# Fewer blocks of 256 rows and more of 512, partly beside the routing, in a convolution and mixture-of-experts kernel

## The chip, the cores and the metric

The kernel runs on one core of a Trainium2 chip. The metric is the device time in microseconds of one execution. Three runs of the kernel before gave 1305.73 (the median), 1305.75 and 1302.89 us. A fourth execution was profiled: it took 1303.41 us, of which the span from the first to the last instruction is 1301.4.

The engines are named as in the profile: PE (TensorE, matrix products; PEld are its weight loads), DVE (VectorE), ACT (ScalarE), POOL (GpSimd, which also issues the scattering transfers) and SP (which issues the plain transfers). A lower-case q (SPq) marks an engine's sequencer. Each engine works through its own list of instructions in order.

## The reference

A causal convolution with softmax weights per head comes first, then a mixture of eight experts, one per token:

```python
# x (8, 3584, 192), 8 heads of 24 channels, 7 taps; w = softmax(weight)
out = einsum('hk,bskhg->bshg', w, windows_of(x))      # convolution
# mixture of experts on the result, D = 192, E = 8, F = 1024
logits = x @ w_gate
local_gate = sigmoid(x @ w_local)
for b in range(B):
    for s in range(S):
        fresh_e = argmax(logits[b, s])
        e = fresh_e if s == 0 or local_gate[b, s] < 0.5 else prev_e
        prev_e = e
        p = softmax(logits[b, s])
        h = maximum(x[b, s] @ w1[e], 0)
        out[b, s] = p[e] * (h @ w2[e])
```

All is in 32-bit floats. There are 28672 tokens. Each keeps the expert of the token before it unless its local gate is below one half, so the choice of expert runs along each sequence.

## The kernel before

**Routing.** The tokens are cut into 16 parts of 1792. For each part, `conv` computes the convolution (per head one product on ACT, L402, then six multiply-and-adds on DVE, L412: 48 a part). `logits` transposes the result on DVE (L595), multiplies it by the gate on PE (L605), copies the products to SBUF on ACT (L610), transposes them again (L613) and puts them in place with 16 small copies on DVE (L621). `route` is then a long row of small DVE instructions which find each token's expert and its place among that expert's tokens. The tokens' rows are scattered by `put` (L802) to a list in DRAM, one list per expert in units of 128 rows: 14 scatters a part, issued by POOL. `table` (L815) computes for a kind of block which expert and which units the blocks of that kind take. A "part" in the change's description is such a part; the parts are counted from 0 in the code.

**Blocks.** The experts' work is done in blocks of rows which all belong to one expert: `blocks` (L919) is the list of them in the order in which PE does them. A single has 128 rows, a pair 256, a block of four 512. A block loads its rows (`load_rows`, 97.5, 195 or 390 KB) and its expert's weights (`load_w`, 1536 KB), both issued by SP three blocks ahead. How many blocks of a kind are surely full after so many parts is known before the run (`_sure`); where a number is only probable (`_likely`, with the rows left over set by LEFT4 and the like), spare blocks at the end make up for a wrong guess. By the constants, before has 28 singles, then 63 pairs, then, when all parts are routed, 13 blocks of four, 4 pairs and 15 singles, with 18 spare singles behind a branch.

**How a block is computed.** For singles and pairs up to the end of the 63 (`FIRST` blocks), `turn` transposes the next block's rows on PE and copies them with ACT to xT, `hidden` does 24 matmuls of 256 columns (for a pair; 64 of the array's rows each, two halves side by side), ACT's relu makes hT, and `output` does 32 matmuls of 192 columns, one scaling by the token's probability on ACT and one on DVE (L1031), and a scatter of each 128 rows to the output by POOL (L1035). From `FIRST` on, `banks.close()` gives the PSUM banks to the late form. There a block of four does its hidden layer by `seven`: sums and differences of halves of the weights (`combine_w`, four POOL subtractions) and of the rows (`combine_x`, five DVE instructions), 44 matmuls of 256 columns instead of 48, and three DVE additions (L1167, L1170, L1180) with relus. `output_late` then does the output in two parts of 256 rows.

**The order of the work.** It is written out by hand: the program's order is each engine's order. Between the pieces of a block, `step(time)` emits instructions of `route` and `conv` until their estimated costs reach `time`. A generator yields its cost after each instruction (0.6 for a convolution's, 0.2 for a small one), or "hop" to give way to the convolution for the rest of that step. Per pair there are steps of 4.8, 1.2 and 3.6. `put` emits one scatter, if one is waiting, and can hang it behind an instruction, so that scatters stand apart. `ensure(i)` loads the rows up to three blocks ahead, and if the parts needed two blocks ahead are not routed or not put, it emits the routing at once. There are no steps in the late form before the change: everything is routed by then.

**Buffers.** Row tiles (y_sb) rotate over four; in the late form the two x tiles and a row tile hold the transposed rows, their combinations, the combined weights and the hidden pieces (`make_room`, L1052), and another row tile is a ring of four blocks' rows (`ring`).

The lines that set the cost of a pair and of a block of four:

```python
        if i < FIRST:
            hT = hidden(n, wbs[i], xT, (1, 1) if i else (0, 0))
            ...
            step(2.4 if i == 0 else 2.1 if n == 1 else 4.8)
            output(n, wbs.pop(i), xgs.pop(i), hT)
            ...
            step(1.3 if n == 1 else 3.6)
            continue
        ...
        if n == KQ:
            hT, at, wt = seven(wbs[i], wt, xT, xc, turn_next, weights_next)
```

Of the kernel before, what the change touches and what calls it, by code (L numbers as in the profile page):

```python
# [17 lines left out]
P = 128  # L18
# [5 lines left out]
UT = 128  # L24
# [41 lines left out]
PAIRED = 63  # L66
LEFT4 = E * (QT // 2 + UT // 8)
LEFT2 = E * (BT // 2 + UT // 8)
# [3 lines left out]
PAST = ONE[-1] * UT + TWO[-1] * BT  # L72
FOUR = _likely(N - PAST, QT, LEFT4)
LOST = FOUR - _sure(N - PAST, QT)
# [7 lines left out]
REST = NU - ONE[-1] - 2 * TWO[-1] - 4 * FOUR - 2 * PAIRS + LOSE  # L82
# [21 lines left out]
def kernel(  # L104
# [14 lines left out]
    ys = ctx.enter_context(tc.tile_pool(name="ys", bufs=4))  # L119
# [5 lines left out]
    hp = ctx.enter_context(tc.tile_pool(name="hp", bufs=1))  # L125
    op = ctx.enter_context(tc.tile_pool(name="op", bufs=2))
# [244 lines left out]
    tab = [cst.tile([P, 3], F32, name=f"tab{k}") for k in range(5)]  # L371
    ends = [cst.tile([P, 1 + E], F32, name=f"ends{k}") for k in range(5)]
    for k in range(5):
        nc.gpsimd.memset(tab[k], 0.0)
        nc.gpsimd.memset(ends[k], 0.0)
# [12 lines left out]
    def row_tile():  # L388
        return ys.tile([P, NB, DG], F32, name="y_sb")

    def conv(g, x_sb):
        y_sb = row_tile()[:, :NT, :]
# [197 lines left out]
    def logits(g, y_sb):  # L590
# [6 lines left out]
        yield "hop"  # L597


        lps = [hps_p.tile([P, TQ * Q], F32, name="hps") for half in range(2)]  # L600
# [14 lines left out]
        lt = sm.tile([P, NT + 2, E + 1], F32, name="lt")  # L615
        for r in range(4):
            for j in range(4):
                t, u = TQ * j, min(TQ * (j + 1), NT)
                at = r // 2 * TQ + t - begin[j]
                e0 = r % 2 * (E + 1)  # L620
                nc.vector.tensor_copy(lt[Q * r:Q * r + Q, t:u, :],  # L621
                                      lq[Q * j:Q * j + Q, at:at + u - t, e0:e0 + E + 1])
                yield 0.12
        return lt

    def route(g):
# [62 lines left out]
        krow = sm.tile([1, 2, P], F32, name="krow")  # L689
# [89 lines left out]
    def tables(g):  # L779
        if ONE[g] > (ONE[g - 1] if g else 0):  # L780
            yield from table(0, g, 1, ONE[g])
        if TWO[g] > (TWO[g - 1] if g else 0):
            yield from table(1, g, 2, TWO[g])
        if g == LAST:
            yield from table(2, g, 4, FOUR, 0)
            yield from table(3, g, 2, PAIRS, 0)
            yield from table(4, g, 1, None)
            yield from fill(g)
# [133 lines left out]
    blocks += [(2, 4, i, LAST) for i in range(FOUR)]  # L922
    blocks += [(3, 2, i, LAST) for i in range(PAIRS)]
    blocks += [(4, 1, i, PADS) for i in range(REST)]
# [40 lines left out]
    def turn(n, xg):  # L965
# [9 lines left out]
        xT = tp.tile([P, KD, BT], F32, name="xT")  # L975
# [13 lines left out]
    def hidden(n, wb, xT, shares=(1, 1)):  # L989
# [4 lines left out]
        for two in range(2):  # L994
            hps = [hps_p.tile([P, 2, BT], F32, name="hps") for half in range(2)]
            for d in range(KD):
                for j in range(2):
                    f0 = (d * 4 + two * 2 + j) * P
                    for half, rows in halves():
                        nc.tensor.matmul(hps[half][:, j, w], lhsT=wb[rows, f0:f0 + P],  # L1000
                                         rhs=xT[rows, d, w], start=(d == 0 and j == 0),
                                         stop=(d == KD - 1), skip_group_check=True)
# [7 lines left out]
    def output(n, wb, xg, hT):  # L1010

        yps = [yps_p.tile([P, 512], F32, name="yps") for half in range(2)]
        for m4 in ([0, 1, 4, 5], [2, 3, 6, 7]):
            for k in range(n):
                for m in m4:
                    for half, rows in halves():
                        nc.tensor.matmul(yps[half][:, k * D:(k + 1) * D],  # L1017
                                         lhsT=hT[rows, m, k * P:(k + 1) * P],
                                         rhs=wb[rows, WA + m * D:WA + (m + 1) * D],
                                         start=(m == 0 and k == 0), stop=(m == FK - 1),  # L1020
                                         skip_group_check=True)
        o_sb = op.tile([P, KT, D], F32, name="o_sb")
        y = [[yps[half][:, k * D:(k + 1) * D] for half in range(2)] for k in range(n)]
        for k in range(n):
            half = nc.scalar.activation(o_sb[:, k, :], y[k][0], Act.Copy, scale=xg[:, k, 0:1])  # L1025
        if n == KT and len(to_put) > NT - 2:
            put(half)

        step(1.2 if n > 1 or st["block"] else 0)
        for k in range(n):  # L1030
# [3 lines left out]
            nc.gpsimd.nop()  # L1034
            sent = nc.gpsimd.indirect_dma_start(  # L1035
                out=out, in_=o_sb[:, k, :], in_offset=None,
                out_offset=bass.IndirectOffsetOnAxis(ap=xg.bitcast(I32)[:, k, IX:], axis=0),
                bounds_check=N - 1, oob_is_err=False)
            tc.declare_no_dep(sent.ins, group="sent", reason="each token has one slot")
            tc.add_to_no_dep_group("sent", sent.ins)  # L1040
# [4 lines left out]
    def ring(i):  # L1045

        if "rows" not in room:
            room["rows"] = row_tile().rearrange("p b d -> p (b d)")
# [3 lines left out]
    def make_room():  # L1052

        one, two = [xs.tile([P, NX, D], F32, name="x_sb").rearrange("p t d -> p (t d)")
                    for _ in range(2)]
        three = row_tile().rearrange("p b d -> p (b d)")
        for name, flat, at, size in (("xT", one, 0, KD * QT), ("xc", one, KD * QT, 4 * HU * P),
                                     ("wt", one, KD * QT + 4 * HU * P, 6 * P),
                                     ("h0", two, 0, 4 * HU * P), ("h1", two, 4 * HU * P, 4 * HU * P),
                                     ("h2", two, 8 * HU * P, 4 * HU * P), ("h3", three, 0, 4 * HU * P)):  # L1060
            room[name] = flat[:, at:at + size]
# [13 lines left out]
    def turn_in(n, at):  # L1075
        xT = room["xT"][:, :KD * n * P].rearrange("p (d s) -> p d s", d=KD)
# [34 lines left out]
    def combine_w(wb):  # L1111


        wt = room["wt"].rearrange("p (k s) -> p k s", k=3)
# [397 lines left out]
```

## Time and profile before

| what | value |
|---|---|
| three runs | 1305.73 us median, 1302.89 to 1305.75 |
| the profiled execution | 1303.41 us |
| its span | 1301.4 us, mean granted PE clock 0.997 |
| last convolution instruction on DVE | ends at 799.9 us |
| last of the 63 pairs on PE | ends at 902.9 us |
| blocks of four on PE | 902.9 to 1168.4 us (13 x 20.42) |

The page of the profile shows for each engine its busy time, and then the span in 40 slices of 32.5 us, one digit each for the busy share in tenths. In the timeline a line gives the start, the length, the engine, the line of the kernel, the operation, its output and inputs, and how many instructions are merged. A matmul on 32-bit floats leaves two records. PE's ends are modelled, so the starts of its instructions are what to measure between. In the table of stretches, each engine has its busy time and, in brackets, its number of instructions. Two more groups, to see what scatters and copies cost:

```profile
L802 POOL DMA_INDIRECT slots<-y_sb,posi x228 | 229.7, 1007 | 203.3 <-ACT xT L986 86.3
L402 ACT ACTIVATE y_sb<-x_sb,c 128x336 f32<-128x336 f32 x112 | 61.7, 578 | 0.0
```

After the number of instructions stand the busy time in us, the mean of one in ns, and the idle time of the engine before them with what ended most of it.

### The profile page before, as it was taken

The numbers are of one execution on the slowest core, as the hardware profiler recorded it, in microseconds if no ns is written. First come the engines' busy times: TensorE is split into PE (matmuls) and PEld (weight loads), VectorE is DVE, ScalarE is ACT, GpSimd is POOL, SyncE is SP. The second block draws the span as 40 slices with busy tenths as digits, with TensorE's granted clock in tenths as the row PEclk, the third lists the DMA queues.
The fourth block names the chain that finished last, engine by engine and source line by source line (L and its number), as shares of the span: only waits on it lengthen the run. The fifth ranks groups of instructions, "written<-read, shape, count | busy, mean of one in ns | idle before, by whom it ended". The sixth has DMA issues, their size and how long they took to land. (4 is left out here: it accounts for less than half of the span.)

```text
span 1301.4 us, 40454 instructions
## 1 busy us (share of the span) xinstructions
PE 1283.3 (99%) x16290; PEld 1218.0 (94%) x16290; DVE 844.9 (65%) x2507; ACT 647.4 (50%) x1458; POOL 523.0 (40%) x577
## 2 busy tenths in 40 slices
PE   8899999999999999999999999999999999999997
PEld 7799999999999999999999999999999999999997
DVE  6989898888989899999998986812333333320000
ACT  5456564545544454444544444344565645544443
POOL 4455352434435344453544535455433343321111
PEclk9999999999999999999999999999999999999999
DMA  5899998757757576675766756556232323324684
GB/s 198 285 353 414 390 387 319 269 189 262 261 207 277 190 278 244 217 275 202 275 238 239 272 202 217 201 209 239 87 120 106 138 92 132 132 85 170 224 320 172
DMA packets 62210, 295.67 MB, mean 227 GB/s; under 512 B 11968, under 2 KB 33783, under 8 KB 44994
## 3 DMA queue, kind: packets, MB, share of 16 engines
q1 hardware_dynamic: 39696, 247.82, 52.7%
q0 software_dynamic: 22320, 45.22, 9.5%
q8 instruction: 130, 2.13, 0.7%
q14 instruction: 62, 0.51, 0.1%
q10 hardware_dynamic: 2, 0.00, 0.0%
HBM read 247.40 MB, written 46.07 MB: 226 GB/s over the span
## 5 line engine op out<-in xcount | busy, mean ns | idle before, releaser
L1017 PE MATMUL yps<-wb,hT 64*128 64x192 f32 x4928 | 426.4, 326 | 2.2 <-DVE o_sb L1031 2.2
L1000 PE MATMUL hps<-xT,wb 64*128 64x256 f32 (+1 forms) x4368 | 421.2, 345 | 1.7 <-DVE at L504 1.2
L1017 PEld LDWEIGHTS yps<-wb,hT 64*128 64x128 f32 x4928 | 403.3, 188 | 3.7 <-DVE o_sb L1031 2.5
L1000 PEld LDWEIGHTS hps<-xT,wb 64*128 64x128 f32 x4368 | 372.3, 187 | 34.7 <-issue 3.6
L412 DVE SCALAR_TENSOR_TENSOR y_sb<-x_sb,c,y_sb 128x336 f32<-128x336 f32 x672 | 375.6, 570 | 28.0 <-ACT y_sb L402 10.0
L802 POOL DMA_INDIRECT slots<-y_sb,posi x228 | 229.7, 1007 | 203.3 <-ACT xT L986 86.3
L1005 ACT ACTIVATE hT<-hps 128x512 f32<-128x512 f32 (+1 forms) x364 | 173.7, 529 | 243.4 <-PE hps L1000 243.3
L1035 POOL DMA_INDIRECT out_dram<-o_sb,xg x154 | 160.4, 1041 | 276.4 <-DVE o_sb L1031 219.0
L1210 DVE SCALAR_TENSOR_TENSOR o_sb<-ps,y_sb,o_sb 128x192 f32<-128x192 f32 x75 | 28.5, 414 | 238.9 <-ACT o_sb L1207 238.9
L1215 POOL DMA_INDIRECT out_dram<-o_sb,y_sb x75 | 77.4, 1032 | 240.9 <-DVE o_sb L1210 230.2
L1197 PE MATMUL ps<-wb,x_sb 64*128 64x192 f32 x1984 | 167.9, 324 | 0.0
L1197 PEld LDWEIGHTS ps<-wb,x_sb 64*128 64x128 f32 x1984 | 162.0, 187 | 0.6
L1025 ACT ACTIVATE o_sb<-yps,xg 128x192 f32<-128x192 f32 x154 | 57.8, 417 | 179.8 <-PE yps L1017 179.8
L986 ACT COPY xT<-xps 64x256 f32<-64x256 f32 (+3 forms) x364 | 138.9, 382 | 10.6 <-PE xps L384 5.1
L1031 DVE SCALAR_TENSOR_TENSOR o_sb<-yps,xg,o_sb 128x192 f32<-128x192 f32 x154 | 58.0, 410 | 73.4 <-ACT o_sb L1025 73.3
L1207 ACT ACTIVATE o_sb<-ps,y_sb 128x192 f32<-128x192 f32 x75 | 28.2, 417 | 103.5 <-PE ps L1197 99.0
L1153 PE MATMUL ps<-x_sb,wb 64*128 64x256 f32 x624 | 73.8, 376 | 0.0
L1153 PEld LDWEIGHTS ps<-x_sb,wb 64*128 64x128 f32 x624 | 59.1, 187 | 7.2
L1104 PE MATMUL ps<-x_sb,wb 64*128 64x128 f32 (+1 forms) x912 | 64.6, 294 | 0.1
L1104 PEld LDWEIGHTS ps<-x_sb,wb 64*128 64x128 f32 x912 | 62.1, 188 | 1.4 <-issue 0.7
L402 ACT ACTIVATE y_sb<-x_sb,c 128x336 f32<-128x336 f32 x112 | 61.7, 578 | 0.0
L1084 ACT COPY x_sb<-xps 64x512 f32<-64x512 f32 (+6 forms) x128 | 59.8, 467 | 2.4
(277 smaller groups left out, 1040.5 us busy)
## 6 DMA issues: line engine op xcount, KB each, us to landing
wb<-in_w_dram SPq DMA_DIRECT2D x119, 1536.0 KB
x_sb<-in_x_dram SPq DMA_DIRECT2D x14, 1920.0 KB
xg<-slots SPq DMA_DIRECT2D x63, 195.0 KB
wb<-in_w_dram SPq DMA_DIRECT2D x12, 512.0 KB
y_sb<-slots SPq DMA_DIRECT2D x13, 390.0 KB
slots<-y_sb,posi POOLq DMA_INDIRECT x228
x_sb<-in_xb_dram SPq DMA_DIRECT2D x4, 768.0 KB
xg<-slots SPq DMA_DIRECT2D x26, 97.5 KB
```

Source lines behind the costliest of these rows:

```text
L402: nc.scalar.activation(cols(h), chans(h, 0), Act.Copy, scale=c[:, h, 0:1])
L412: nc.vector.scalar_tensor_tensor(cols(h), chans(h, k), c[:, h, k:k + 1], cols(h), Alu.mult, Alu.add)
L802: ins = nc.gpsimd.indirect_dma_start(out=slots[:, :], in_=rows, in_offset=None, out_offset=bass.IndirectOffsetOnAxis(ap=to, axis=0)).ins
L986: copied = nc.scalar.copy(a, b)
L1000: nc.tensor.matmul(hps[half][:, j, w], lhsT=wb[rows, f0:f0 + P], rhs=xT[rows, d, w], start=(d == 0 and j == 0), stop=(d == KD - 1), skip_g ...
L1005: relu = nc.scalar.activation(hT[:, m:m + 2, w], hps[half][:, :, w], Act.Relu)
L1017: nc.tensor.matmul(yps[half][:, k * D:(k + 1) * D], lhsT=hT[rows, m, k * P:(k + 1) * P], rhs=wb[rows, WA + m * D:WA + (m + 1) * D], start= ...
L1035: sent = nc.gpsimd.indirect_dma_start(out=out, in_=o_sb[:, k, :], in_offset=None, out_offset=bass.IndirectOffsetOnAxis(ap=xg.bitcast(I32)[ ...
L1104: nc.tensor.matmul(hps[:, half, j, :], lhsT=wb[rows, f0:f0 + P], rhs=xT[rows, d, :], start=(d == 0 and j == 0), stop=(d == KD - 1), skip_g ...
L1153: ins = nc.tensor.matmul(to[:, half, j, :], lhsT=b[rows, j * P:(j + 1) * P], rhs=a[rows, :], start=(first and j == 0), stop=True, skip_gro ...
L1197: ins = nc.tensor.matmul(yps[:, half, k * D:(k + 1) * D], lhsT=h[two][rows, side, j, k * P:(k + 1) * P], rhs=wb[rows, WA + f * D:WA + (f + ...
L1215: sent = nc.gpsimd.indirect_dma_start(out=out, in_=o_sb[:, k, :], in_offset=None, out_offset=bass.IndirectOffsetOnAxis(ap=xg.bitcast(I32)[ ...
```

## The change

The 63 pairs become 44. After them come 18 blocks of four which are taken as the parts are routed (parts 9 to 14, table kind 2, cumulative numbers 1, 4, 8, 11, 15, 18 in `MID`), then 4 more when all is routed, 5 pairs and 15 singles, with 14 spare singles. The routing thus runs on beside the late form. For that:

- `seven` and `output_late` get steps of their own, `SIDE` = 2.4, 5.4, 2.0 and 1.8: ahead of the addition to h11, ahead of the output, and ahead of the DVE scalings of each of the two output parts. What a step overran is taken off the next (`over`), and in the late form each routing instruction is charged 0.05 more.
- The logits' products on PE need a PSUM tile. In the late form they use one of the block's own (`bank`), behind the first output part, at the earliest a block after their transposes were emitted ("pe" in place of the first "hop").
- From the seventh part on (`aside`), the 16 small copies of `logits` go to ACT, four at a time with a "hop" after each four.
- The second scatter of each 256 rows of output is held back (`held`) and hung behind a matmul of the next block; some puts hang behind matmuls instead of ACT instructions; puts in the late form move.
- The late form no longer takes x tiles: its pieces lie in the tile that `hots` used, in five small row tiles and in hT. Row tiles rotate over four up to part 7 and over three from then on.
- `combine_x` is cut in two so that its last two results can wait for hT in the first block of four; `ensure` is called inside `seven`.

The diff, cut:

```diff
-PAIRED = 63
+PAIRED = 44
+LEFTM = E * (QT // 2 + UT // 2)
...
+MID = [_likely((g + 1) * PT - PAST, QT, LEFTM) if TWO[g] == TWO[-1] else 0
+       for g in range(LAST)]
...
-    def row_tile():
-        return ys.tile([P, NB, DG], F32, name="y_sb")
+    def row_tile(g):
+        at = g % 4 if g < NARROW else (g + 1) % 3
+        return ys[at].tile([P, NB, DG], F32, name="y_sb")
...
-        yield "hop"
-        lps = [hps_p.tile([P, TQ * Q], F32, name="hps") for half in range(2)]
+        yield "pe"
+        if late_p:
+            both = st["bank"].tile([P, 2, 512], F32, name="ps")
+            lps = [both[:, half, :TQ * Q] for half in range(2)]
+        else:
+            lps = [hps_p.tile([P, TQ * Q], F32, name="hps") for half in range(2)]
...
+        aside = g > EARLY + 2
...
-                nc.vector.tensor_copy(lt[Q * r:Q * r + Q, t:u, :],
-                                      lq[Q * j:Q * j + Q, at:at + u - t, e0:e0 + E + 1])
-                yield 0.12
+                if aside:
+                    nc.scalar.copy(dst, src)
+                else:
+                    nc.vector.tensor_copy(dst, src)
+                    yield 0.12
+            if aside:
+                yield "hop"
...
+        if MID[g] > (MID[g - 1] if g else 0):
+            yield from table(2, g, 4, MID[g], MID[g - 1])
...
+            if k == 0:
+                deliver(o_sb[:, 0, :], xg, 0)
+            else:
+                held.append(lambda ins, k=k: deliver(o_sb[:, k, :], xg, k, ins))
...
-    def seven(wb, wt, xT, xc, turn_next, weights_next):
+    def seven(wb, wt, xT, xc, rows_then, turn_next, weights_next):
...
-        times(yb, s1, t1, True)
+        ins = times(yb, s1, t1, True)
+        if held:
+            held.pop(0)(ins)
+        rows_then()
...
+        if st["block"] > FIRST:
+            step(SIDE[0], early=1)
         nc.vector.tensor_tensor(h11, wbk, h11, op=Alu.add)
...
+            if n == KQ:
+                step(SIDE[2 + part], late_p[0] if part == 0 else None)
...
+    SIDE = (2.4, 5.4, 2.0, 1.8)
...
-    def step(time):
+    def step(time, bank=None, early=0, force=False):
...
+        if st["due"]:
+            go = (not late_p and st["block"] < FIRST - 1
+                  or bank is not None and (force or st["since"] < st["block"]))
+            if go:
+                st["due"], st["bank"] = False, bank
+        time += st["over"]
...
-                time -= c
+                time -= c + 0.05 if go and late_p else c
+        st["over"] = min(time, 0) if late_p else 0
...
+        if n == KQ:
+            step(SIDE[1])
```

## The prediction

> **What bounds the kernel now.** I read the page's engine lines and slices first, then TensorE's timeline in the middle and in the late stage, then the busy times of single blocks, then VectorE beside GpSimd. The chain of waits is of no use here: it holds only the last scatter.
>
> ```profile
> PE 1283.3 (99%) x16290; PEld 1218.0 (94%) x16290; DVE 844.9 (65%) x2507; ACT 647.4 (50%) x1458; POOL 523.0 (40%) x577
> PE   8899999999999999999999999999999999999997
> DVE  6989898888989899999998986812333333320000
> ```
>
> TensorE is full from the second slice to the last. VectorE is nearly full up to slice 27 of 40 (about 850 us; convolution and routing) and lightly used after. So the end moves only if TensorE gets less work, or if VectorE makes it wait.
>
> TensorE's timeline, first two blocks of 256 rows, then one of 512 (start, length, line, count of records; a matmul leaves two records):
>
> ```profile
> 613.06 5.42 PE L1017 MATMUL yps<-wb,hT 64*128 64x192 f32 x64
> 618.32 5.35 PE L1000 MATMUL hps<-xT,wb 64*128 64x256 f32 x48
> 623.50 0.40 PE L384 MATMUL xps<-ident,xg 64*128 64x64 f32 x8
> ...
> 634.39 5.42 PE L1017 MATMUL yps<-wb,hT 64*128 64x192 f32 x64
> ```
> ```profile
> 943.75 2.75 PE L1153 MATMUL ps<-x_sb,wb 64*128 64x256 f32 x24
> ...
> 949.79 1.89 PE L1153 MATMUL ps<-x_sb,wb 64*128 64x256 f32 x16
> 951.52 0.64 PE L384 MATMUL xps<-ident,y_sb 64*128 64x64 f32 x16
> 951.99 1.08 PE L1153 MATMUL ps<-x_sb 64*128 64x256 f32 x8
> ...
> 964.17 1.03 PE L1153 MATMUL ps<-x_sb,wb 64*128 64x256 f32 x8
> ```
>
> Two blocks of 256 rows take 634.39 - 613.06 = 21.33 us, without a gap. The block of 512 takes 964.17 - 943.75 = 20.42. It does the same rows with 44 hidden matmuls of 256 columns (`seven`) in place of 48. The gain is 0.91 us for each 512 rows.
>
> Busy times over one such stretch each (length, then PE, PEld, DVE, ACT, POOL):
>
> ```profile
> 602.40:623.73 21.33, 21.33 (x247) 20.09 (x243) 19.55 (x86) 10.08 (x24) 8.08 (x9) 1.00 0.52 183
> 943.75:964.17 20.42, 20.42 (x234) 19.24 (x234) 7.01 (x12) 11.24 (x15) 7.20 (x8) 1.00 0.33 117
> ```
>
> Beside two pairs VectorE is already 19.55 of 21.33 busy, of which only four scalings (2 x 0.74) belong to the blocks. A block of 512 brings 7.0 us of its own, so 13.4 are left for routing there.
>
> **What the Trainium skill says.** "TensorE: Matmul & The Clock Gate", Back-to-back issue gap: a warm matmul follows the last after N/2.4 + 2.5 ns. That is 109 ns for 256 columns; the trace has 48 records in 623.50 - 618.32 = 5.18 us, so 108. Hence TensorE's time is its columns, and four matmuls (eight records) less are 0.87 us by the page, 0.91 by the trace, which I use. The same page, under "Architectural detail: the array is 16× 32×32, not 1× 128×128", says that ScalarE and VectorE are strict first in, first out; a late instruction delays everything written behind it (no row of before shows that at a price, as VectorE is never late for TensorE in mid-kernel). "SBUF — State Buffer", Who interferes with whom: a VectorE instruction with two SBUF inputs and a GpSimd instruction that reads SBUF exclude each other. This trace shows it, on VectorE and on GpSimd, in the one place where such work meets:
>
> ```profile
> 900.61 0.93 DVE L1131 TENSOR_TENSOR x_sb<-x_sb 128x256 f32<-128x256 f32 x1 [1.21 <-ACT x_sb L1084]
> 901.58 0.84 DVE L1132 TENSOR_TENSOR x_sb<-x_sb 128x256 f32<-128x256 f32 x1
> 902.45 0.83 DVE L1133 TENSOR_TENSOR x_sb<-x_sb 128x256 f32<-128x256 f32 x1
> ...
> 961.06 0.42 DVE L1131 TENSOR_TENSOR x_sb<-x_sb 128x256 f32<-128x256 f32 x1
> ```
> ```profile
> 901.34 0.79 POOL L1120 TENSOR_TENSOR x_sb<-wb 128x256 f32<-128x256 f32 x1
> 902.21 0.80 POOL L1122 TENSOR_TENSOR x_sb<-wb,x_sb 128x256 f32<-128x256 f32 x1
> ```
>
> Beside GpSimd the same subtraction takes 0.83 to 0.93 us instead of 0.42: about 0.44 lost for each GpSimd subtraction met.
>
> **The change part by part.**
>
> *Blocks on TensorE.* By the constants, before has 28 singles, 63 pairs, 13 blocks of 512, 4 pairs, 15 singles (the last 18 are spare and skipped). After has 28, 44, 18 + 4, 5, 15. In the instructions, 256-column hidden matmuls fall from 2180 to 2144, which is 9 x 4; all else on TensorE is unchanged in sum, logits included. 9 x 0.91 = **8.2 us less**. The blocks beside routing are filled by a guess of how many whole units exist (LEFTM); a wrong guess would run empty blocks. Counted from the reference's own choices for these inputs, the tables at parts 9 to 14 find 3, 5, 11, 12, 15, 20 such units where 1, 4, 8, 11, 15, 18 are asked, and 15 singles remain in both kernels. So the change does what it says, and no spare runs.
>
> *VectorE in sum.* Nine more blocks of 512 for 18 pairs: 9 x 7.0 - 18 x 0.74 = +50 us. Four more tables (13 in place of 9) of some 4 us each (L821 to L884 in the timeline at 617.8): +16. Logit copies of ten parts leave: 160 x 0.2 = -32. Net +34 on 845, beside TensorE. As it has 80 us idle between 215 and 850 (554.73 of 635 busy) and more later, the sum hides; only its place can hurt.
>
> *VectorE in each late block.* With the order of instructions in the changed kernel and durations from the rows of before (convolution 0.583 us apart: 14 in 8.18), routing and convolution in the 16 blocks of 512 that carry any come to 9.2 to 12.1 us in the ten full ones (heaviest the sixth, with the transposes of the logits), and 0 to 8.3 in the rest. So a full block has 7.0 + 10.9 = 17.9, heaviest 19.1, of 20.42. To that comes the meeting with GpSimd: four `combine_w` subtractions per block, which so far mostly lay beside an idle VectorE. Lower bound 0 (beside additions from PSUM), nearest row 0.44 each, upper bound their whole 0.73: 0 to 2.9 us per block; I take 1.8. Full blocks are then at 19.7, the heaviest at 20.9.
>
> *Where a late VectorE stops TensorE.* In the late block from its start: the addition to h11 can begin at 5.46 (949.21), the one to h22 ends at 7.8, and at 8.24 (951.99) the next product into that PSUM tile needs it. That leaves 0.43 us. Ahead of h11 in the queue now stand the last scaling of the block before (from 0.95), 1.7 us of routing ahead of that, and 2.3 behind it. Fed at full rate, VectorE is at 9.2 after h12, does 7 us plus 1 to 1.5 of meeting, two scalings at about 18, `combine_x` to 20.5, routing to 22.2 (1.8 of the next block), scalings to 2.5, routing to 4.8: h11 is in time by 0.6. A convolution also waits for ScalarE's first product of its head (L402), which in this place stands behind the four xT copies ending at 14.0 (957.78): up to 1 us in some blocks. In the sixth block it and the 8.1 us of its side work push h11 to about 6.7, and TensorE stops for some 1 us. I take 1 for this, 0.3 for each of five other full blocks: **2.5 us of stalls**; bounds 0 and 8.
>
> *Copies of logits on ScalarE.* From the seventh part on, 16 a part; ScalarE does 64x128 in 0.26 and 64x256 in 0.365, so a 36-element one is about 0.18: 2.9 us a part, four at a time. In pairs ScalarE idles 50% and has free stretches of 2 us; the cover is those. In late blocks it goes from 11.2 by 1.1 (L402) and 0.7 to 13 of 20.4. Zero; if one group falls ahead of a copy of h11, whose slack is 1.3 us, a few tenths.
>
> *GpSimd.* 36 more subtractions (26 us) and puts, now behind matmuls. A late block holds 4 x 0.74, four deliveries and five puts at about 1.3 each: 14.6 of 20.4. The second delivery of a block waits for a product of the next; behind it stand puts, for which the row loads on SP wait. The loads are two blocks (40 us) ahead, so zero. The same holds for the first of the four groups of the last part: its rows are loaded in the 17th late block and turned in the 18th.
>
> *Buffers.* The 512-row blocks move from the x buffers to others (hot, small xg tiles, hT), and row tiles rotate over three from part 8; the start of convolution g already required that g-3 was put. Zero. Weight loads fall by nine; DMA is 0.3 to 0.9 busy. Zero.
>
> Sum: 1301.4 - 8.2 + 2.5 = 1295.7 span; with the 2.0 us around it (1303.41 - 1301.4) 1297.7. The profiled execution lies 2.3 under the median of the runs and 0.5 over the fastest; their mean is near 1304.4, 1298.7 from there. I forecast **1298**.
>
> **Rivals.**
> *The stalls take the gain.* Each of the ten full blocks loses 0.7 us, by meeting GpSimd near the upper bound and L402 late each time: 7 of the 8.2, so 1303. For it: only 0.43 us of slack. Against: blocks with tables and light routing, where VectorE recovers.
> *Slower: VectorE becomes the bound of the late blocks beside routing.* Its place is the in-order queue ahead of h11. If a full block costs it 7.0 + 11.6 (the planner's own quota, 2.4 + 5.4 + 2.0 + 1.8) + 2.9 + 0.5 of waits for ScalarE = 22.0, then the ten full blocks are each 1.6 over TensorE's 20.42: +16 - 8.2, about 1312 from the mean of the runs. The lead of the routing then cannot help, for the delay sits in the block's own additions. It decides from 8.2 / 10 = 0.82 us per block on. For it: 19.55 of 21.33 was busy already, with less work of the blocks. Against: the quota overstates small operations (routing L697 to L774: 8.1 us measured for 9.4 charged).
> *No stalls at all*: 1301.4 - 8.2 + 2 = 1295; inside the forecast's case.
>
> **How the numbers follow.** What a measurement of this kernel tells from no change is about 0.3%, 3.9 us. Forecast with zero to 4 us of stalls: 0.71, at 1294 to 1301. Gain eaten: 0.15, at 1301 to 1307. Slower: 0.14, above 1308, most near 1312. Faster is the first case and 0.01 of the second, 0.72; the same 0.13; slower 0.15 with the top of the second. The range is 1294 to 1304: below it 0.04, above it 0.15 at most.
>
> **What would show it.** Late blocks of 20.4 us from about 700 us on (902.91 - 19 x 10.67), 22 of them; TensorE's idle time within them under 4 us, ended by VectorE's addition to h11 or h22, mostly in the sixth and seventh; VectorE at 18 to 20 us in full blocks, its convolutions or `combine_x` stretched where GpSimd subtracts. Periods of 21 us or more in many blocks, or gaps where rows are waited for, would prove it wrong.

## The result and the profile after

Of each kernel there are twenty runs. The kernel before took 1304.5 us (median, 1301.84 to 1307.87), the changed kernel 1300.88 (1297.88 to 1304.85). The ratio is 0.9971, with a 95% interval from 0.9962 to 0.9979. The forecast was 1298, its range 1294 to 1304. The profiled execution of the changed kernel has a span of 1296.3 us, against 1301.4 before: 5.1 less in the two profiles, 3.6 in the two medians. The changed kernel's profiled execution, 1298.23 us, is the second lowest of its twenty.

The page after, its engine lines and the two slices that were shown of before:

```profile
PE 1276.7 (98%) x16218; PEld 1232.7 (95%) x16218; DVE 909.4 (70%) x2513; ACT 704.0 (54%) x1573; POOL 546.0 (42%) x615
PE   9899999999999999999999999999999999999997
DVE  6989898888888888798888888988468434310000
```

TensorE is busy 6.6 us less and is full as before. VectorE now works up to slice 32 (about 1040 us): its row stays at 8 where it was at 9, so the routing is stretched over more of the span, as the change intends.

TensorE's timeline, one late block (a block of 512 rows) beside routing; its first line is the block's start, its last the start of the next:

```profile
694.20 2.76 PE L1194 MATMUL ps<-xT,wb 64*128 64x256 f32 x24
...
702.43 1.09 PE L1194 MATMUL ps<-xT,xg 64*128 64x256 f32 x8
703.35 1.03 PE L1194 MATMUL ps<-xT,wb 64*128 64x256 f32 x8
704.22 10.57 PE L1243 MATMUL ps<-wb,hot 64*128 64x192 f32 x128
714.62 2.76 PE L1194 MATMUL ps<-xT,wb 64*128 64x256 f32 x24
```

714.62 - 694.20 = 20.42 us, with VectorE 19.59 busy in it. The next table gives the time of such stretches, each from the start of a late block to the start of the next: length, then PE, PEld, DVE, ACT and POOL with their numbers of instructions, the granted clock, the DMA share and GB/s. They are the first, second, third, fourth, sixth, seventh, eighth and ninth late block:

```profile
694.20:714.62 20.42, 20.42 (x236) 19.52 (x235) 19.59 (x30) 11.64 (x16) 13.53 (x15) 1.00 0.39 141
714.62:736.76 22.14, 22.14 (x331) 20.86 (x330) 20.00 (x33) 12.98 (x20) 14.05 (x15) 1.00 0.41 137
736.76:757.98 21.22, 20.67 (x236) 20.03 (x235) 16.22 (x28) 16.66 (x35) 6.23 (x8) 1.00 0.59 210
757.98:779.06 21.08, 20.67 (x235) 20.33 (x234) 17.71 (x58) 11.44 (x16) 8.63 (x10) 1.00 0.34 114
...
799.48:819.90 20.42, 20.42 (x236) 20.38 (x235) 16.23 (x27) 12.66 (x18) 10.66 (x13) 1.00 0.43 142
819.90:843.88 23.98, 22.80 (x331) 21.55 (x330) 23.32 (x39) 13.13 (x20) 14.49 (x15) 1.00 0.37 122
843.88:864.51 20.63, 20.63 (x236) 20.03 (x234) 17.00 (x29) 15.71 (x33) 6.20 (x7) 1.00 0.34 113
864.51:884.93 20.42, 20.42 (x236) 20.38 (x234) 16.27 (x57) 11.43 (x16) 6.87 (x9) 1.00 0.35 117
```

Blocks with some 331 records on PE hold the logits' 96; those take 1.73 us in a block of 512, and before they were in pairs. Taken off, the excess over 20.42 is a stall: third block 0.80, fourth 0.66, seventh 23.98 - 20.42 - 1.73 = 1.83, eighth and twelfth 0.2 each. All 22 late blocks together take 457.92 us. Unstalled they would take 22 x 20.42 - 0.2 (the last is a little shorter) + three logits of 1.73 to 1.75 = 454.2. So the stalls are **3.7 us**, half of them in one block.

What TensorE waited for in that stretch (total, times, longest). These idle times add up to 2.2 us only, since PE's ends are modelled; how long the stalls are is read from the starts:

```profile
PE ps L1194 <- DVE hot L1216: 0.9, 2, 0.5
PE xps L392 <- DVE hot L1213: 0.7, 1, 0.7
PE ps L1194 <- issue: 0.6, 1, 0.6
```

The first two are the additions to h22 (L1216) and h11 (L1213) which came late in the fourth and seventh block. "issue" is the third block, where the profile names no releaser. There ScalarE's timeline shows it (block start 736.76):

```profile
737.60 0.89 ACT L638 COPY lt<-lq 32x36 f32<-32x36 f32 x4
738.50 0.58 ACT L411 ACTIVATE y_sb<-x_sb,c 128x336 f32<-128x336 f32 x1
738.98 0.99 ACT L1200 COPY hot<-ps 128x1024 f32<-128x1024 f32 x1
```

Four small copies of logits (L638) and a first product of the convolution stand ahead of the copy of h11 (L1200). It begins 2.22 us after the block's start; in the sixth block it begins 1.15 after (800.63 - 799.48). It ends at 739.97, and TensorE's next product starts at 740.07: until then it couldn't go on into that PSUM tile.

The seventh block is late from the sixth on. VectorE's timeline, from the sixth's transposes of the logits (L604) to the seventh's addition to h11 (L1213):

```profile
808.62 3.15 DVE L604 STREAM_TRANSPOSE z<-y_sb 128x768 f32<-128x768 f32 x4
814.02 5.19 DVE L421 SCALAR_TENSOR_TENSOR y_sb<-x_sb,c,y_sb 128x336 f32<-128x336 f32 x8 [2.25 <-ACT y_sb L411]
819.20 0.74 DVE L1258 SCALAR_TENSOR_TENSOR o_sb<-ps,y_sb,o_sb 128x192 f32<-128x192 f32 x2
...
820.77 1.43 DVE L1172 TENSOR_TENSOR xg<-xT 128x256 f32<-128x256 f32 x1
...
825.25 2.27 DVE L421 SCALAR_TENSOR_TENSOR y_sb<-x_sb,c,y_sb 128x336 f32<-128x336 f32 x4
827.43 1.22 DVE L1213 TENSOR_TENSOR hot<-xps,hot 128x1024 f32<-128x1024 f32 x1
```

The addition begins 827.43 - 819.90 = 7.53 us into the block, where 5.5 would do. VectorE had waited 2.25 us for the first product of a new convolution (L411), which on ScalarE stands behind the four xT copies:

```profile
810.71 2.79 ACT L1124 COPY xT<-xps 128x512 f32<-128x512 f32 x4
813.41 1.05 ACT L411 ACTIVATE y_sb<-x_sb,c 128x336 f32<-128x336 f32 x2
```

And the row subtraction L1172 takes 1.43 us there; such a subtraction took 0.42 in the kernel before. So three causes were to be told apart: ScalarE's small copies, the convolution's first products behind other ScalarE work, and GpSimd's subtractions beside VectorE.

### The profile page after: what moved, and what is told of

Its sections match the earlier page's. It is cut to its first block, busy times and chain, and to the rows that moved or that the text cites. A ratio compares the mean times of both kernels' runs of the same rounds, so it can differ in the third digit from the quotient of the medians.

```text
span 1296.3 us, 40433 instructions
## 1 busy us (share of the span) xinstructions
PE 1276.7 (98%) x16218; PEld 1232.7 (95%) x16218; DVE 909.4 (70%) x2513; ACT 704.0 (54%) x1573; POOL 546.0 (42%) x615
## 3 DMA queue, kind: packets, MB, share of 16 engines
q8 instruction: 130, 2.13, 0.7%
## 4 chain that ended last, share of the span: by engine, by line
PE 95%; DVE 2%; issue 1%; POOL 1%; DMA 1%; ACT 0%; POOLq 0%; SPq 0%; DVEq 0%
PE yps L1043 24%; PE hps L1024 23%; PE ps L1243 23%; PE ps L1194 13%; PE ps L1144 5%; PE xps L1194 3%; PE xps L392 2%; PE hps L618 1%; POOL slots L824 1%; PE hps L242 1%; PE hps L187 0%; PE ps L618 0%; DMA xg<-slots 0%; DMA slots<-y_sb,posi 0%; DVE hot L584 0%
## 5 line engine op out<-in xcount | busy, mean ns | idle before, releaser
L1043 PE MATMUL yps<-wb,hT 64*128 64x192 f32 x3712 | 323.8, 326 | 0.5 <-issue 0.4
L1024 PE MATMUL hps<-xT,wb 64*128 64x256 f32 (+1 forms) x3456 | 319.3, 336 | 1.6 <-DVE at L513 1.2
L1024 PEld LDWEIGHTS hps<-xT,wb 64*128 64x128 f32 x3456 | 284.9, 187 | 24.8 <-issue 2.9
L1043 PEld LDWEIGHTS yps<-wb,hT 64*128 64x128 f32 x3712 | 304.9, 188 | 2.6 <-issue 2.0
L1243 PE MATMUL ps<-wb,hot 64*128 64x192 f32 x3616 | 303.9, 323 | 0.0
L1243 PEld LDWEIGHTS ps<-wb,hot 64*128 64x128 f32 x3616 | 296.4, 187 | 0.7 <-issue 0.6
L1010 ACT COPY xT<-xps 64x256 f32<-64x256 f32 (+4 forms) x288 | 106.8, 371 | 10.1 <-PE xps L392 5.7
L1124 ACT COPY xT<-xps 64x512 f32<-64x512 f32 (+6 forms) x168 | 86.2, 513 | 2.2
L1194 PE MATMUL ps<-xT,wb 64*128 64x256 f32 x704 | 84.8, 376 | 0.0
L1194 PEld LDWEIGHTS ps<-xT,wb 64*128 64x128 f32 x704 | 73.7, 187 | 1.6 <-issue 0.3
L1144 PEld LDWEIGHTS ps<-xT,wb 64*128 64x128 f32 x960 | 68.2, 188 | 0.2 <-issue 0.2
L411 ACT ACTIVATE y_sb<-x_sb,c 128x336 f32<-128x336 f32 x112 | 62.9, 580 | 0.5
```

The source lines that it names most:

```text
L411: nc.scalar.activation(cols(h), chans(h, 0), Act.Copy, scale=c[:, h, 0:1])
L1010: copied = nc.scalar.copy(a, b)
L1024: ins = nc.tensor.matmul(hps[half][:, j, w], lhsT=wb[rows, f0:f0 + P], rhs=xT[rows, d, w], start=(d == 0 and j == 0), stop=(d == KD - 1), ...
L1043: ins = nc.tensor.matmul(yps[half][:, k * D:(k + 1) * D], lhsT=hT[rows, m, k * P:(k + 1) * P], rhs=wb[rows, WA + m * D:WA + (m + 1) * D], ...
L1124: copied = nc.scalar.copy(a, b)
L1144: nc.tensor.matmul(hps[:, half, j, :], lhsT=wb[rows, f0:f0 + P], rhs=xT[rows, d, :], start=(d == 0 and j == 0), stop=(d == KD - 1), skip_g ...
```

## The experiments

All edits are to the changed kernel, if nothing else is said. "Excess" is a late block's time over 20.42 us, the logits' 1.73 to 1.75 included where it has them (second, seventh and eleventh; in e3 and e4 the twelfth in place of the eleventh). The first four kernels ran on one chip, where the kernel before took 1304.16 us (11 runs).

**First products earlier (e1).** Each head's first product goes to ScalarE two heads ahead, in place of one.

```diff
         first(0)
+        first(1)
...
-            if h + 1 < H:
-                first(h + 1)
+            if h + 2 < H:
+                first(h + 2)
```

> Each head's first product on ScalarE is issued two heads ahead instead of one; nothing else changes. In the changed kernel the 22 late blocks take 457.9 us on TensorE: 449.0 at 20.42 each, 5.3 for three sets of logits, 3.6 of stalls (0.8 in the third, 0.7 in the fourth, 1.8 in the seventh). Theory A (VectorE is late because its convolution waits for ScalarE behind the four xT copies, 2.25 us in the sixth block, 2.3 in the third): those waits go to under 0.5, the stalls of the fourth and the seventh block fall below 0.5 each, the 22 blocks take about 455.5. Theory B (each block is given more routing than VectorE has time for): the stalls stay above 3 us.

The fourth block's 0.66 is gone (0.0); the third keeps 0.79, the seventh 3.58. So earlier first products are enough to take away the fourth's stall; they are not its only cause, since e2 and e3 take it away too. The seventh's did not go this way: there the convolution is a new one, and even its first two products are issued behind the xT copies (VectorE's wait was 2.26 us again). All late blocks took 457.27 us, so 3.0 us of stalls are left and theory A holds for the fourth block alone. The span was 1298.9 nevertheless, 2.6 more than the changed kernel's, and one line of what TensorE waited for after the late blocks says why:

```profile
PE ps L1145 <- DMA wb<-in_w_dram: 2.8, 1, 2.8
```

A single of the tail waited for its weights (L1145, here one line further down). In the changed kernel's profile that stretch has no such wait; in the others it has between none and 3.7 us in all. That spread hides a gain of half a microsecond, so what follows is read from the late blocks, not from one span.

**No subtractions on GpSimd (e2).** The weights' sums and differences are computed in the first late block alone and left as they are, so four GpSimd instructions a block are left out, and the hidden layer with them is not the reference's.

```diff
+        if "once" in room:
+            yield from (None, None, None, room["wt"])
+            return
+        room["once"] = True
```

> Left out: GpSimd's subtractions of the weights from the second late block on (four a block)[...]. Theory A, part lock (VectorE's subtraction of rows takes 1.43 instead of 0.42 in every late block, a convolution 0.74 instead of 0.58 beside them): the row subtraction is back at 0.42 to 0.46, convolutions at 0.58, VectorE gains about 1.5 us a block, the stall of the seventh block falls from 1.8 below 0.7, the 22 blocks take about 456. If the lock is no cause, the stalls stay at 3.6 (457.9). The third block's 0.8 should stay either way, since it is ended by a ScalarE copy.

The seventh falls from 3.57 to 1.97, which is the logits and 0.2; the fourth to 0.01; the third keeps 0.77. VectorE still waits 2.25 us in the sixth. These are theory A's figures, although the convolution's start was left as it is. The stretch of 315.18 us from the second late block on, in the changed kernel and then in this one (columns as above):

```profile
714.62:1029.80 315.18, 313.04 (x3771) 307.54 (x3770) 240.69 (x578) 187.84 (x297) 159.44 (x173) 1.00 0.41 136
```
```profile
716.49:1031.67 315.18, 314.67 (x3793) 302.31 (x3792) 212.66 (x577) 189.44 (x300) 115.50 (x113) 1.00 0.40 137
```

With one VectorE instruction fewer (577 for 578) VectorE is 28.0 us less busy. Over the some 15 late blocks of the stretch that is 1.9 us each: the price of meeting GpSimd's subtractions. One place of it, the row subtraction, in the changed kernel and then, as the same instruction, in this one (shortest, median and longest in ns):

```profile
L1172 DVE TENSOR_TENSOR xg<-xT x22: 841/1428/1435, 692.9 to 1129.3; 128x256 f32<-128x256 f32 x22
```
```profile
L1176 DVE TENSOR_TENSOR xg<-xT x22: 424/425/836, 694.7 to 1128.8; 128x256 f32<-128x256 f32 x22
```

**Copies of logits back on VectorE beside late blocks (e3).** ScalarE keeps those of the parts routed beside pairs.

```diff
-        aside = g > EARLY + 2
+        aside = g > EARLY + 2 and not late_p
```

> The small copies of logits go back to VectorE for the parts whose logits are computed beside late blocks (three parts); before that they stay on ScalarE. Theory A, part copies (four of them stand ahead of the copy to h11 on ScalarE in the third late block and hold it by 0.9 us): the third block's stall goes to 0, and its long wait of the convolution shrinks by 0.9. But VectorE gets 3.5 us more per part, so the rival (too much routing for VectorE) expects larger stalls in the fourth and the seventh and later blocks, over 4 us in all.

Nearly every stall is gone: 454.42 us for the 22 late blocks, with excesses of 1.73 and twice 1.75 for the logits and two of 0.1. In the list of what TensorE waited for between 696.33 and 1150.74 us there is not one line, where the changed kernel had three. VectorE is busier than it was (first line the changed kernel, second this one, both ending at 1029.80, which is 1.35 us into the next block in the second):

```profile
694.20:1029.80 335.60, 333.45 (x4003) 327.06 (x4002) 260.28 (x607) 199.48 (x313) 172.97 (x187) 1.00 0.40 136
```
```profile
696.33:1029.80 333.47, 333.47 (x4017) 319.46 (x4016) 270.22 (x657) 189.85 (x268) 170.85 (x184) 1.00 0.40 136
```

270.2 us in place of 260.3, and no stall: that VectorE had simply too much to do falls. The third block is plain, the copies no longer stand ahead of h11's. For the seventh, VectorE's timeline of this kernel shows another order (block starts 800.15 and 820.66):

```profile
809.36 1.78 DVE L421 SCALAR_TENSOR_TENSOR y_sb<-x_sb,c,y_sb 128x336 f32<-128x336 f32 x3
811.17 2.70 DVE L604 STREAM_TRANSPOSE z<-y_sb 128x768 f32<-128x768 f32 x3
...
820.18 0.57 DVE L604 STREAM_TRANSPOSE z<-y_sb 128x384 f32<-128x384 f32 x1
820.68 1.13 DVE L421 SCALAR_TENSOR_TENSOR y_sb<-x_sb,c,y_sb 128x336 f32<-128x336 f32 x2
...
826.15 1.22 DVE L1213 TENSOR_TENSOR hot<-xps,hot 128x1024 f32<-128x1024 f32 x1 [1.31 <-PE xps L1194]
```

On VectorE each copy is charged 0.12 to its step; on ScalarE it was charged nothing. So the transposes reach further into the steps, and VectorE takes up the new convolution at 820.68, a step later than in the changed kernel; its first product, issued at 816.32, is done long before. VectorE now waits for TensorE (1.31) at the addition to h11. Here the moved copies thus acted twice: by standing on ScalarE, and by what they did to the order. That the charge of zero did the second is argued from the costs: the edit also takes out the "hop" after each four copies, and no run separates the two.

The run's span is 1296.6 us all the same, no less than the changed kernel's 1296.3. Its first late block starts 2.1 us later (696.33 against 694.20), although the instructions up to there are the same, and what stands behind the late blocks takes 1.7 us more.

**All three (e4).** Two heads ahead as in e1, the first four copies a step later, and three of the four subtractions moved ahead in `seven`; seven runs.

```diff
+        if late_p:
+            yield "hop"
...
+        wt = weights_next()
+        for _ in range(3):
+            next(wt)
```

> Three moves together: first products two heads ahead; in the late form the logit copies begin one step later, behind the copies to h11 and h12; three of the four weight subtractions stand directly ahead of the last two products with s4 and s5, so that they run beside VectorE's additions from PSUM. Theory A: stalls under 1 us in all, the 22 blocks take 454.5 to 455.3, the span falls by 2.6 to 3.4 against the changed kernel's 1296.3, ratio to before about 0.995. Theory B: stalls of 3 us or more remain, ratio 0.997.

1299.83 us, ratio 0.9967 (0.9956 to 0.9978): no better than the changed kernel as far as this tells. The stalls fell by about one microsecond, to some 2.6, not below 1. The third is at 0, but the fourth has 0.48, and so have the ninth and the fourteenth: a step later, the last group of copies falls ahead of the copy of h11 in the block after. ScalarE's timeline of the fourth (block start 757.00):

```profile
757.97 0.89 ACT L641 COPY lt<-lq 32x36 f32<-32x36 f32 x4
758.89 1.01 ACT L1203 COPY hot<-ps 128x1024 f32<-128x1024 f32 x1
```

The stall thus moved with the copies, which shows that it is theirs. The seventh keeps 1.2 beyond its logits. A miss: VectorE's wait for the new convolution's first product (2.25 us) was not touched by any of the three edits, and the subtractions only moved.

The experiments from here on ran on three other chips, where the kernel before took 1332.6 to 1335.0 us. Their profiles hold gaps that the first chip's do not have (the last section shows them), so each is read against the kernel before as it ran beside it on the same chip.

**The start of a convolution ahead of the xT copies (e6, and again e10).** As e1, and the first products of the next convolution are issued at the end of each late step.

```diff
         st["over"] = min(time, 0) if late_p else 0
+        if late_p:
+            start_conv()
```

> The changed kernel with the first product of each head issued two heads ahead, and a new convolution's first two products already issued at the end of the late step before it, hence ahead of the four xT copies. Theory (the 1.84 us stall of the seventh late block arises because a new convolution in the sixth waits for first products that stand behind the xT copies): the seventh's excess over 20.42 falls from 3.57 to under 2.3 (1.73 are logits), the fourth's stays near 0 as with two heads ahead, the third's 0.8 (logit copies ahead of h11's copy) stays. Rival (VectorE simply has too much work in the sixth, with the transposes and the meeting with GpSimd): the seventh stays at 3.3 or more.

> The kernel of e6 once more, as its late blocks held gaps of ScalarE that the changed kernel does not have. Theory (a new convolution's first products stood behind the xT copies): the seventh late block's excess falls from 3.57 to under 2.3, the fourth's stays near 0, the third's 0.8 stays; late blocks in 455 to 456.5 us. Rival (too much work for VectorE in the sixth): the seventh stays at 3.3 or more. In e6 it read 3.11, which tells nothing while the third, without any edit to it, read 0.84 and the second 2.6.

The seventh's excess was 3.11 and 3.10: neither theory's number. What it is made of can be read in e10's two timelines, VectorE's and TensorE's (sixth block from 823.19, seventh from 844.06; lines are one further down than in the changed kernel):

```profile
835.83 6.20 DVE L422 SCALAR_TENSOR_TENSOR y_sb<-x_sb,c,y_sb 128x336 f32<-128x336 f32 x8
...
850.26 1.22 DVE L1214 TENSOR_TENSOR hot<-xps,hot 128x1024 f32<-128x1024 f32 x1
```
```profile
852.76 1.13 PE L1195 MATMUL ps<-xT,xg 64*128 64x256 f32 x8 [0.26 <-DVE hot L1217]
853.70 1.06 PE L1195 MATMUL ps<-xT,wb 64*128 64x256 f32 x8
855.36 5.47 PE L1244 MATMUL ps<-wb,hot 64*128 64x192 f32 x64 [0.60 <-DVE hot L1227]
```

The wait of 2.25 us ahead of the eight multiply-and-adds is gone. Not all of it is won, since they now take 6.20 us in place of 5.19: two of GpSimd's subtractions fall beside them in place of one. The addition to h11 begins 6.20 us into the block in place of 7.53, and the product behind h22 starts 8.70 into it, 0.46 late against 8.24. The rest, some 0.8, is an addition (L1227) that began 1.4 us after the one ahead of it had ended; the profile names no instruction that released it. So moving the start takes 1.3 us off the lateness, and e2's leaving out the subtractions takes 1.5 (7.53 to 6.03). Both make the seventh late, by 2.0 us together (7.53 against 5.5), and taking away either was enough to push it most of the way under VectorE's slack. Whether this kernel comes under 2.3 without the gaps of this chip was not tried.

**The small part of the change alone (e7).** The kernel before, with only its logits' copies on ScalarE from the seventh part on (the same lines as in the change).

> The kernel before with only the one small part of the change: the copies of logits go to ScalarE from the seventh part on, beside pairs only. Prediction (free, hidden in ScalarE's idle half beside pairs; VectorE's relief is off the path): same as before, within 0.5 us of its median, ratio 0.9990 to 1.0010. Rival (ScalarE's copies delay the first products and thereby the routing or the evictions also beside pairs): 1 us or more slower, ratio above 1.001.

1340.5 us, ratio 1.0053 (1.0028 to 1.0077): slower, as the rival had it. But TensorE's longest waits are again of the new kind (`issue` 11.4 us in 24 places, and three waits of up to 3.0 for a relu that ScalarE began late), and gaps of up to 1.9 a pair also stand in pairs before the first moved copy. Since the kernel before was not profiled on this chip, its gaps can't be taken off. The run shows that the copies bring nothing beside pairs here; what they cost on the first chip stays open.

**The copies back, timed (e5, e9, e12, with the changed kernel beside it in e11).** The kernel of e3, six runs each.

> The changed kernel with the small copies of logits back on VectorE for the three parts whose copies fall into late blocks, now timed. Its profile had 22 late blocks in 454.42 us in place of 457.92. Theory (the 3.6 us of stalls come from instructions on ScalarE standing in the wrong place, and nothing is given back elsewhere): 3.5 us under the changed kernel's 1300.9, so about 1297.4, ratio to before 0.9935 to 0.996. Rival (the runs lose elsewhere, at the waits for weights in the singles, what the late blocks gain): 1299.5 to 1301, ratio above 0.9965.

> The kernel of e5 once more. In e5's call the kernel before took 1332.6 us and ScalarE showed gaps of up to 5 us that no wait explains, so its ratio also holds what such gaps cost. Theory (3.6 us of stalls removed, nothing given back) where the kernel before takes 1304 to 1305: late blocks in 454.4 us again, median 1297 to 1298.5, ratio 0.9940 to 0.9955, interval below 0.9965. Rival (the timed gain is lost at the weight loads of the singles): 1299.5 or more, ratio above 0.9962.

> The changed kernel itself once more, beside e12. Theory (the 28 us by which the kernel before was longer in the calls of e5 to e10 come from gaps in ScalarE's supply of instructions, at fixed places in its list, and more small ScalarE instructions mean more such gaps): where the kernel before takes about 1333, this one gains less than the 3.6 us of the first comparison or nothing, ratio 0.996 to 1.001; where it takes about 1304.5, ratio 0.9965 to 0.9975 as before. Rival (the gaps hit all kernels alike): ratio 0.997 in both.

> The kernel of e5 beside e11. Theory (the small copies on ScalarE in the late blocks cost 3.6 us of stalls): 3 to 4 us under e11 where the kernel before takes about 1304.5, that is near 1297.5, and more than that where it takes about 1333. Rival (the late blocks' gain is lost at the weight loads of the singles): within 1.5 us of e11.

| run | this, us | before, us | ratio | interval |
|---|---|---|---|---|
| e5 copies back | 1325.70 | 1332.61 | 0.9931 | 0.9904 to 0.9958 |
| e9 copies back | 1325.17 | 1334.99 | 0.9929 | 0.9908 to 0.9950 |
| e11 changed kernel | 1326.63 | 1333.73 | 0.9944 | 0.9926 to 0.9963 |
| e12 copies back | 1324.43 | 1333.73 | 0.9928 | 0.9911 to 0.9946 |

On each of the three chips the kernel with the copies back has the lowest median of those that ran more than once. But over the changed kernel, which ran beside it on one of them, it is lower only by 2.2 us in medians of six runs whose ranges overlap; there the late blocks took 459.90 us (e12) and 461.70 (e11). On the first chip it has one run, 1298.44, and the changed kernel's profiled execution took 1298.23. That it beats the kernel before is shown, that it beats the changed one by the 3.5 us of its late blocks is not. The theory of e11 fell: the changed kernel gains more on such a chip (7.1 us), not less; its rival fell too, as 0.997 lies outside the interval. A reason could be that it has 19 pairs fewer, and pairs lose more to the gaps there; the kernel before was not profiled on those chips, so this is argued only.

**42 pairs (e8).** The kernel of e5 with one more block of 512 for two pairs.

> The kernel of e5 with 42 pairs in place of 44, so one more block of 512 for two pairs, beside the routing of parts 8 and 9. Theory of the sum (0.91 us for each block of 512, while VectorE keeps up): 0.9 us under e5, about 1296.5. Rival (routing starts the last part later relative to the blocks, so that it has to be emitted at once ahead of one block, and the lump of VectorE's work stops TensorE): 1 to 6 us above e5, with an excess of more than 2 us in one block near the end of the routed ones.

1327.99 us (16 runs), ratio 0.9966 (0.9951 to 0.9980), 2.3 above e5. The 23 late blocks hold 2.5 us more excess than e5's 22, spread over the first thirteen (waits for the addition to h22 and gaps), not in one block near the end. So the rival's size came, not its place. One block more gave nothing on this chip.

## Why the prediction was right, and where not

- *Fewer columns on TensorE, 8.2 us*: right. Late blocks beside routing take 20.42 us where nothing is late, the pair 10.67, TensorE's records fall by 72 (36 matmuls), and no spare block ran. The formula that the prediction took from the Trainium skill ("TensorE: Matmul & The Clock Gate", Back-to-back issue gap) is given there for an isolated matmul, with other figures for a stream of weight loads and matmuls; this kernel's stream fits it nevertheless, with 108 ns for 256 columns. The first late block starts at 694.20, not near 700, because the 19 pairs taken off hold three parts' logits, which 19 x 10.67 leaves out; the gain is the same.
- *Stalls, 2.5 us*: 3.7 in the profile. Here lies the error of the sum: 1301.4 - 8.2 + 3.7 = 1296.9, where 1296.3 was measured; half a microsecond comes from an earlier start, since the changed kernel's first late block starts 0.5 us before the same point of the kernel before (694.20 against 694.70). That half is chance: in e2 and e3, where the instructions up to there are those of the changed kernel, the block starts at 696.07 and 696.33.
- *The sixth block's late h11, 1 us*: right in cause (transposes of logits, a first product behind the xT copies, and the meeting), mis-sized. The wait for the first product was 2.25 us, not up to 1, since a new convolution started there; the stall was 1.8 and showed a block later.
- *0.3 in each of five other full blocks*: wrong in shape. Most full blocks lose nothing, even with VectorE 20.00 us busy in 22.14. The slack takes what is under it; 0.66 in the fourth went with earlier first products (e1), and also without the subtractions (e2) or with the copies back (e3). That the fourth and the seventh add up to 2.5 us (0.66 + 1.83), as 1 + 5 x 0.3 does, is luck.
- *Copies on ScalarE, zero, a few tenths if a group falls ahead of h11's copy*: this step failed. The group did fall there, with a first product behind it: 0.8 in the third block. In the eighth and twelfth it fell there without one: about 0.2 each, also gone in e3. Together these are the 1.2 us that the sum lacked. A copy took 0.219 us by its own row (0.18 was estimated), four of them 0.89. And they moved the routing against the blocks, which e3 undid.
- *Meeting with GpSimd, 1.8 us a block*: right, 1.9 (e2). The Trainium skill ("SBUF — State Buffer", Who interferes with whom) has GpSimd's reads and a VectorE instruction with two SBUF inputs exclude each other; e2 shows that they do meet and what it costs here. The nearest row had given 0.44 us for one meeting; the row subtraction loses 1.0 (1.43 against 0.42).
- *The in-order queues*, for which the Trainium skill's "TensorE: Matmul & The Clock Gate", under "Architectural detail: the array is 16× 32×32, not 1× 128×128", was named: the traces of after, e1 and e10 agree and give it a price, which before did not show: 2.25 us of VectorE idle for one product behind four copies on ScalarE.
- *VectorE as the bound (the rival on the other side)*: it did not come. Full blocks had VectorE at 16 to 20 us, not 22, but for the stalled seventh (23.32 of 23.98).
- *VectorE in sum*: right, once the meeting is added. The two pages differ by 64.5 us (909.4 against 844.9); 34 and 1.8 in each of 16 blocks make 63.
- *The total*: the sum stood against the profile, and there was 1.2 us too little stall in it. The medians differ by 3.6 us, 1.5 less than the two profiles; waits outside the late blocks, such as the tail's for weights (none in the changed kernel's profile, 2.8 us in e1), vary by this much from run to run. So 1300.88 lies just inside the 1294 to 1301 that went with 0 to 4 us of stalls. That the range held it says little, since it reached to half a microsecond under the kernel before; the term-by-term sum is the test. And 3.6 us is a little less than the 3.9 that the prediction took as the least that can be told; it is told here because of the twenty runs of each kernel.

## What to carry to other kernels

A small instruction moved to an engine that idles half the time is not free: look up what is behind it in that engine's queue at the place where it lands, and give it a charge in any hand-written schedule, or it can move the rest. Where a stage has a slack per block, sum up the lateness of all causes within one block and compare it with the slack, in place of giving each block a small mean loss; stalls then show up in one or two blocks, and taking away one of several causes can remove most of them. A gain of a few microseconds is read from the stage it concerns, since transfers elsewhere can vary by as much.

## What the runs showed of the hardware

On the three chips of e5 to e12 the kernel before took 28 to 30 us more than in the first comparison (1332.6 to 1335.0 us against 1304.5). In the profiles taken there the instructions last as long as on the first chip, but engines stand still where the profile names no instruction that they wait for ("issue", or "remote" as below). ScalarE's timeline of e9, a late block, and of the same kernel in e3:

```profile
725.63 1.06 ACT L1227 ACTIVATE hot<-hot 128x1024 f32<-128x1024 f32 x1
728.91 1.02 ACT L1228 ACTIVATE hot<-ps 128x1024 f32<-128x1024 f32 x1 [2.22 <-remote]
729.84 2.79 ACT L1124 COPY xT<-xps 128x512 f32<-128x512 f32 x4
```
```profile
705.57 1.06 ACT L1227 ACTIVATE hot<-hot 128x1024 f32<-128x1024 f32 x1 [0.33 <-DVE hot L1226]
706.56 1.03 ACT L1228 ACTIVATE hot<-ps 128x1024 f32<-128x1024 f32 x1
```

The gap of 2.22 us stands ahead of the same instruction in e5, on another chip. Between 290 and 720 us such gaps of some 0.8 to 3.3 us come at the same places in ScalarE's list in e5 and e9 (ahead of its 408th, 498th, 588th, 665th, 742nd, 827th, 904th and 981st computing instruction, among others), so about every 80 instructions, ahead of xT copies as of relus. That looks like the supply of instructions and not like a wait of the program, but no record names it. The page's DMA queue named "instruction" has the same 130 packets (2.13 MB) in e3 and e9 and does not tell the engines apart, so it does not settle this. In the changed kernel's own profile on such a chip (e11, span 1325.3) the 29 us more lie 11.9 in the 28 singles, 9.2 in the 44 pairs, 3.8 in the late blocks and 4.2 in what stands before and after.
